# Stores of folded weight blocks held back, and the first pair's outputs moved to ScalarE

## The chip, the cores and the metric

One core of a Trainium2 chip runs the whole program. The metric is device microseconds of one execution, the median of three runs. The engines named here are PE (matmuls; PEld is its weight load), DVE (VectorE), ACT (ScalarE), POOL (GpSimd) and SP (SyncE, which here issues nearly every DMA). Each engine works through its instructions strictly in the order of the program.

## The reference

```python
# attention: q, k, v are (8, 8, 576, 64); the bias depends on head and positions alone
scores = q @ k.T / sqrt(64) + bias          # bias = relu(x @ w1 + b1) @ w2
attn = softmax(scores)
x = (attn @ v).transpose(0, 2, 1, 3).reshape(4608, 512)
# then a gated block, with no nonlinearity but the product
a = x @ moe_w1                               # (4608, 1024)
b = x @ moe_w2                               # (4608, 1024)
out = ((a * b) @ moe_w3) @ moe_w_out         # (4608, 512)
```

## The kernel before

The program first computes attention (about 440 us), then folds the two last weights into one, `moe_w3 @ moe_w_out` (1024 x 512, eight blocks of 128 rows, called `folded[ft]`), and then does the gated block. All fp32 factors are kept as a high and a low part, and a product is three matmuls (high by high, low by high, high by low).

The 4608 tokens are cut into six pairs of two tiles of 384 tokens (`CH`). For each pair the loop goes over the eight blocks `ft` of the hidden dimension; `n` counts the 48 steps, and `start(n)` is the planned time of a step.

**The first pair (`p == 0`, n = 0 to 7)** is computed plainly, since the weights of a cheaper scheme are still being made. In each step PE does, for tile `c` and then for tile `d`, two groups of twelve matmuls (`plain`, lines 802 to 814, into the PSUM banks X and Y) and nine matmuls of the down product of the step before (`down`, line 971, into the six banks `oc0` to `od2`). ACT copies X out (line 829), DVE multiplies Y by that copy (line 832, which frees Y for the next group), ACT and DVE split the product (lines 820 and 823). Beside this, ACT, DVE and POOL turn the int64 input weights `moe_w1` and `moe_w2` into fp32 parts (`fetch_w`, `base_w`, `sums_w`: the input lands in one of two tiles `wi` by a DMA of line 189, ACT reads it in line 197, DVE goes on in lines 207, 211 and 221, POOL in line 215), and load and combine the next pair's inputs (`split_x`: loads in lines 719 and 427, DVE lines 742 and 745, ACT line 751).

**The later pairs (n = 8 to 47)** use seven products in place of eight (`product`, line 785, in the order 2, 1, 6, 5, 7, 3, 4 of `AT_P`, all into X and Y) with copies and sums in `evict` (lines 836 to 854), and a seven-product form of the folded weight as well (`outward`, line 913, which reads tiles `fs` loaded from DRAM by line 911). The folded weight gets there through the DRAM arrays `f_d[k]`, k = 0 to 3, of eight slots each. `put_f(k)` (line 878) makes sums of two blocks and stores them (lines 899 and 900), and it also stores the plain blocks themselves: slot 0 and slots 3 and 6 for the high and the low part (lines 897 and 898), and slot 7 for one k (line 902).

**The last down products of the first pair** fall into step n = 8: nine matmuls for `d` at 2.1 us and nine for `c` at 8.4 us after its start (`AT_D`, line 770), among the seven products. `store` (line 987) copies each of the six banks to SBUF (tile `xB0`; two of the six copies on DVE, four on ACT) and SP stores them to `out0` (line 996). Only then are the banks and the SBUF under them free: the tiles `gh`, `gl` and `fs` of the later pairs and the banks of `outward` lie where they were (`first.close()`, `out_ps.close()` after the line 1135).

**What sets the order.** The steps of PE, ACT, DVE and POOL are put into a list with planned times (`at`, `put`), and `drive` emits them sorted by time; these four engines keep that order. SP is not among them: a list scheduler places a DMA on SP as soon as its model finds it ready, and of several ready ones the one emitted earlier. So the plain blocks' stores, which `put_f` emits last, are issued long before the rest of `put_f`, once the blocks exist. Eight semaphores serve all DMAs in turn.

Of the kernel before, what the change touches and what calls it, by code (L numbers as in the profile page):

```python
# [17 lines left out]
P = 128  # L18
# [112 lines left out]
def relpos_attention_moe(  # L131
# [18 lines left out]
    nc = tc.nc  # L150
# [3 lines left out]
    DO = out0.shape[1]  # L154
# [3 lines left out]
    NF = DF // P  # L158
# [4 lines left out]
    def f(ap):  # L163
        return ap.bitcast(F32)
# [80 lines left out]
    def put(plan, steps, *times):  # L245

        def one():
            next(steps, None)
        for at in times:
            plan.append((at, len(plan), one))  # L250
# [113 lines left out]
    for i in range(2):  # L364
        t = att.enter_context(tc.tile_pool(name=f"sums{i}", bufs=1)).tile([P, 64], F32, name=f"sums{i}")
# [112 lines left out]
    later = []  # L478
# [5 lines left out]
    later = [e[:3] for e in later]  # L484

    plan = [e for e in later if e[0] < 0.0]
    later = [e for e in later if e[0] >= 0.0]
# [6 lines left out]
    with ExitStack() as pro:  # L494
# [29 lines left out]
        def reach(G):  # L524

            return (G + 1) * GR - 1, S - 1 - G * GR
# [9 lines left out]
        for G in range(NGRP):  # L536
            n = max(reach(G)) + 1
# [60 lines left out]
    later = [e for e in later if e[0] >= t_s]  # L598
# [16 lines left out]
    f_d = [dram.tile([P, 8, 2, 2 * P], F32, name=f"f_d{k}") for k in range(NF // 2)]  # L615
    ups, base = {}, {}
    pairs = {p: dict(x=[None, None]) for p in range(NPR)}
# [53 lines left out]
    folded, wacc, w3 = {}, {}, {}  # L671
# [65 lines left out]
    def split_x(p, i):  # L737

        xr, rb, flat = load_x(p, i, xs, p == 1 and i == 0)
        yield  # L740
        for n in range(2):
            nc.vector.tensor_tensor(flat[:, n * W2:(n + 1) * W2], flat[:, n * W2:(n + 1) * W2], rb[:, n], op=ALU.mult)
            yield
        for o, x, y in ((4, 1, 0), (1, 3, 1), (5, 3, 4), (6, 2, 5)):
            nc.vector.tensor_tensor(xr[:, o], xr[:, x], xr[:, y], op=ALU.subtract)
            yield
        x = xb[(p + 1) % 2].tile([P, 2, 7, CH], F32R, name=f"xS{i}")
        pairs[p]["x"][i] = x
        places = (slice(1, 3), slice(2, 4)), (slice(0, 6, 5), slice(0, 2)), (slice(3, 5), slice(4, 6)), (6, 6)
        for o, y in places:  # L750
            nc.scalar.activation(x[:, 0, o], xr[:, y], AF.Copy)
            yield
        for o, y in places:
            nc.vector.tensor_tensor(x[:, 1, o], xr[:, y], f(x[:, 0, o]), op=ALU.subtract)
            yield
# [11 lines left out]
        dict(b=(9.80, "ACT"), B=(10.70, "DVE"), c=(11.20, "ACT"), C=(11.80, "DVE")),  # L767
        dict(a=(3.20, "ACT"), A=(4.40, "DVE")),
    )
    AT_D = {"d": 2.1, "c": 8.4}  # L770
    AT_U = {"c": 0.0, "d": 6.25}
    AT_G = {"p": 2.1, "g": 4.2, "h": 4.8, "l": 5.4}
    AT_D0 = {"c": 4.16, "d": 10.41}
# [104 lines left out]
    def put_f(k):  # L878

        (ha, la), (hb, lb) = folded[2 * k], folded[2 * k + 1]  # L880
        s = cva.tile([P, 4, 2 * P], F32, name="wi")
        fa, fb = [cva.tile([P, DO], F32, name="wmag") for i in range(2)]
        for o, x in ((fa, (ha, la)), (fb, (hb, lb))):
            nc.vector.tensor_tensor(o, f(x[0]), f(x[1]), op=ALU.add)
            yield
        a0, a1, b0, b1 = fa[:, 0:2 * P], fa[:, 2 * P:DO], fb[:, 0:2 * P], fb[:, 2 * P:DO]
        for o, x, y, op in (
            (2, a1, b1, ALU.add), (1, a0, a1, ALU.subtract), (0, s[:, 2], a0, ALU.subtract), (3, b0, s[:, 0], ALU.subtract),
        ):
            nc.vector.tensor_tensor(s[:, o], x, y, op=op)  # L890
            yield
        h = bg.tile([P, 4, 2 * P], F32R, name="big")
        nc.scalar.activation(h, s, AF.Copy)
        yield
        nc.vector.tensor_tensor(s.bitcast(F32R), s, f(h), op=ALU.subtract)
        for m, (x, a, b) in enumerate(((f(h), ha, hb), (s, la, lb))):
            nc.sync.dma_start(f_d[k][:, 0, m], f(a[:, 0:2 * P]))
            nc.sync.dma_start(f_d[k][:, 3:7:3, m], f(b).rearrange("p (s n) -> p s n", s=2))
            nc.sync.dma_start(f_d[k][:, 1:3, m], x[:, 0:2])
            nc.sync.dma_start(f_d[k][:, 4:6, m], x[:, 2:4])  # L900
            if k == order(NPR - 1)[-1] // 2:
                nc.sync.dma_start(f_d[k][:, 7, m], f(a[:, 2 * P:DO]))
        yield

    def load_f(k, j, n, plain=False):
        if plain:
# [80 lines left out]
    def store(j, t):  # L987
        if not spare:
            spare.append(x0p.tile([P, 2 * NT, DO], F32, name="xB0"))
        o = spare[0][:, NT * "dc".index(j) + t]  # L990
        if t == 1:
            nc.vector.tensor_copy(o, pairs[0]["o", j, t])
        else:
            nc.scalar.copy(o, pairs[0]["o", j, t])
        r0 = "cd".index(j) * CH + t * P
        nc.sync.dma_start(out0[r0:r0 + P, :], o)

    def at(time, step, *args):
        later.append((time, len(later), lambda: step(*args)))
# [6 lines left out]
    t_f = t_s + 11.12 + (2 * NF - 1) * PACE_F  # L1006
    for i in range(2 * NF):
        hf, t = divmod(i, NF)
# [28 lines left out]
    def start(n):  # L1037
        m = max(n - NF, 0)
        return t_f + STEP0 * min(n, NF) + STEP * m + EXTRA * (m % 2)

    def order(p):
        return [ft for m in range(NF // 2)[::1 if p % 2 == 0 else -1] for ft in (2 * m, 2 * m + 1)]

    for k in range(NF // 2):
        t0 = t_f + (101.0, 94.0, 80.5, 73.5)[k]
        put(later, put_f(k), *(t0 + d for d in (0.0, 0.9, 1.8, 2.4, 3.0, 3.6, 4.1, 5.6)))

    here, past = None, {}
    for n in range(NPR * NF):
        p, s = divmod(n, NF)  # L1050
        ft = order(p)[s]
        t0, t1 = start(n), start(n + 1)
        cs = dict(at=(p, ft), odd=n % 2)
        if p == 0:
            for j, u in AT_U.items():
                for m in range(2):
                    at(t0 + u + 2.08 * m, plain, cs, j, m)
                for k, d in AT_G.items():
                    if n == 0 and k + j == "gc":
                        d = AT_GC  # L1060
                    at(t0 + u + d, gate, cs, k + j)
            for j in "cd":
                t2 = t1 + (AT_D0 if n + 1 < NF else AT_D)[j]
                at(t2, down, cs, j)
                if ft == NF - 1:
                    for t in range(NT):
                        at(t2 + 2.1 + 0.6 * t, store, j, t)
            if ft in (4, 6):
                put(
                    later, split_x(1, int(ft > 4)), t0 - 6.0, t0 + 8.45, t0 + 9.45, *(t0 + 11.6 + 0.5 * d for d in range(4)),  # L1070
                    *(t1 + 2.0 + 0.55 * d for d in range(8)),
                )
            continue
        for k, d in AT_P.items():
            if n == NF and k == "4":
                d += 1.05
            at(t0 + d, product, cs, k)
        for k, d in AT_E.items():
            at(t0 + d, evict, cs, k)
        if s > 1:  # L1080
            put(later, load_w(p, ft), t0 - 2 * STEP + 0.3)
        if p < NPR - 1 and s in (0, 4):
            times = [start(n + d) + t for d, t in AT_X]
            put(later, split_x(p + 1, s // 4), start(n - 1) + 6.1, *times)
        if s % 2 == 0:
            continue
        m, k = s // 2, ft // 2
        last = n + 1 == NPR * NF
        for q in range(2):
            for key, (d, _) in (AT_SL if last else AT_S)[1 - q].items():  # L1090
                d = 5.4 + 0.1 * d if n == NF + 1 and key in "sS" else d
                at(start(n + (0 if last else q)) + d, sums_g, key)
        if last:
            at(past["2"] + 1.3, load_f, k, "1", 4, True)
            at(t0 + 4.5, join)
            for i, (o, w, g) in enumerate(((0, 0, 0), (2, 2, 0), (1, 0, 1), (3, 2, 1), (1, 3, 2), (3, 1, 2), (0, 3, 5), (2, 1, 5))):
                at(t0 + 10.55 + 1.05 * i, finish, o, w, g, i < 4)
                if i > 3:
                    at(t0 + 11.70 + 1.05 * i, last_of, p, o)
            continue  # L1100
        at(start(n + 1) + 0.50, sums_g, "R")
        for j, (q, d, e) in AT_O.items():
            tb = start(n + 1 + q)
            at(tb + d, outward, m, j)
            if e is not None:
                at(tb + e, gather, m, j, dict(zip("16753", (0, 1, 2, 3, 1)))[j])
            if here != k and j in F_BY:
                at(past[j] + 1.3 if j in past else start(NF + 1) + 5.5 + 0.05 * (q * STEP + d), load_f, k, *F_BY[j])
            past[j] = tb + d
        here = k  # L1110
        if m == NF // 2 - 1:
            for o, (q, d) in enumerate(((1, 0.2), (1, 7.6), (2, 1.1), (1, 4.5))):
                at(start(n + 1 + q) + d, complete, p, o)
# [91 lines left out]
```

## Time and profile before

| | |
|---|---|
| runs | 1051.98, 1052.49, 1053.36 us; median 1052.49 us |
| profiled execution | 1052.97 us, of which 1050.8 us lie from the first to the last instruction |
| busy, share of the span | PE 1020.6 us (97%), DVE 922.3 (88%), ACT 580.2 (55%), POOL 320.1 (30%) |
| granted clock of PE, mean | 0.995 |
| chain that ended last | PE 74%, DVE 10%, issue 7%, ACT 3%, DMA 3%, POOL 3% |
| DMA moved | 236.22 MB, 225 GB/s over the span |

A time in a row below is counted from the span's first instruction. In a timeline a row is one instruction, or several alike in a row (`x12`), with its start and its length; in square brackets stands how long the engine was idle before it and what ended that. A letter q behind an engine means its queue: a DMA issue, or a wait on semaphores. The first pair's steps run from about 493 to 595 us, step n = 8 from 595 us.

### The profile page before, as it was taken

Reading aid. Unit: us, or ns where it says so; the run is one execution under the profiler, and the core shown is the slowest. Engines: PE = TensorE matmul, PEld = TensorE weight load, DVE = VectorE, ACT = ScalarE, POOL = GpSimd, SP = SyncE. Lnnn points to the kernel's source line nnn. Section 1 sums busy time; section 2 is a strip of 40 time slices with the busy share of each in tenths; the row PEclk is TensorE's granted clock in tenths of the full one; section 3 lists DMA queues with packets and bytes.
Section 4 is the critical chain, followed back from the end, with each engine's and each line's share of the span. In section 5 each row is a group of like instructions: output and inputs, shape, how many; then the busy total and the mean of one; then the engine's idle time right before and its main releaser. Section 6 shows DMA issues by size and latency. Waiting matters only on the chain.

```text
span 1050.8 us, 34041 instructions
## 1 busy us (share of the span) xinstructions
PE 1020.6 (97%) x14094; PEld 837.6 (80%) x14094; DVE 922.3 (88%) x1616; ACT 580.2 (55%) x1250; POOL 320.1 (30%) x344
## 2 busy tenths in 40 slices
PE   7979999999999999999999989999999999999998
PEld 2346666666666666688899979999999999999998
DVE  8989999999999999998889958897887888787665
ACT  6957887877877788856454442334325333242421
POOL 0027885883778288674220000000000000000000
PEclk9989999999999999999999999999999999999999
DMA  7987777776776766367867788758648766764752
GB/s 215 298 236 230 209 213 222 217 211 200 211 220 186 202 189 192 115 167 239 321 220 279 242 327 291 267 181 317 230 159 300 261 219 216 277 227 146 250 196 90
DMA packets 109675, 236.22 MB, mean 225 GB/s; under 512 B 23376, under 2 KB 60624, under 8 KB 102736
## 3 DMA queue, kind: packets, MB, share of 16 engines
q1 hardware_dynamic: 109088, 234.02, 68.2%
q8 instruction: 111, 1.82, 0.7%
q14 instruction: 44, 0.36, 0.1%
q10 hardware_dynamic: 432, 0.02, 0.0%
HBM read 181.68 MB, written 52.31 MB: 223 GB/s over the span
## 4 chain that ended last, share of the span: by engine, by line
PE 74%; DVE 10%; issue 7%; ACT 3%; DMA 3%; POOL 3%; SPq 0%; DVEq 0%; ACTq 0%; POOLq 0%
PE X L797 16%; PE Y L797 12%; PE acc L442 11%; PE s L346 10%; PE ox L919 9%; DVE ts L357 4%; PE o L919 4%; PE bacc L566 3%; DVE pt L392 3%; PE X L811 3%; PE Y L811 2%; POOL w3s L688 2%; PE oc L980 1%; PE od L980 1%; DMA wi<-in_moe_w_dram 1%
## 5 line engine op out<-in xcount | busy, mean ns | idle before, releaser
L382 ACT ACTIVATE pp<-ts,mx 128x576 f32<-128x576 f32 x256 | 196.1, 767 | 39.9 <-DVE mx L357 38.9
L442 PE MATMUL acc<-pt,v 32*64 32x128 f32 (+1 forms) x9216 | 212.9, 294 | 2.4 <-issue 2.4
L442 PEld LDWEIGHTS acc<-pt,v 32*64 32x64 f32 x9216 | 160.0, 130 | 69.2 <-issue 44.8
L346 PE MATMUL s<-k,q 64*128 64x288 f32 (+1 forms) x1280 | 194.3, 441 | 6.7 <-DVE mx L357 4.7
L797 PE MATMUL X<-xS,wS 128*128 128x384 f32 x960 | 194.2, 336 | 2.7 <-DVE wos L840 1.3
L357 DVE CUSTOM_DVE_ANT_0 ts<-s,nb 128x576 f32<-128x576 f32 x256 | 182.4, 737 | 5.3 <-PE s L346 5.1
L392 DVE STREAM_TRANSPOSE pt<-pp 128x1152 f32<-128x1152 f32 x128 | 175.3, 1371 | 2.3 <-ACT pp L382 1.4
L797 PEld LDWEIGHTS X<-xS,wS 128*128 128x128 f32 x960 | 169.6, 188 | 4.2 <-ACT wos L844 1.9
L346 PEld LDWEIGHTS s<-k,q 64*128 64x128 f32 (+1 forms) x1280 | 91.1, 176 | 74.8 <-issue 35.8
L797 PE MATMUL Y<-xS,wS 128*128 128x384 f32 x720 | 145.4, 336 | 0.0
L844 ACT COPY wos<-X 128x384 f32<-128x384 f32 x80 | 38.4, 481 | 167.3 <-PE X L797 165.8
L797 PEld LDWEIGHTS Y<-xS,wS 128*128 128x128 f32 x720 | 127.0, 188 | 0.5 <-ACT wos L844 0.2
L334 POOL COPY v<-v 64x512 f32<-64x512 f32 (+1 forms) x160 | 87.5, 567 | 117.3 <-DMA v<-in_v_dram 98.3
L862 ACT ACTIVATE gh<-gr 128x768 fp32r<-128x768 f32 (+1 forms) x79 | 58.2, 760 | 81.4 <-DVE gr L867 69.2
L919 PE MATMUL ox<-gh,fs 128*128 128x384 f32 x380 | 97.0, 336 | 1.6 <-ACT gh L862 1.6
L930 DVE TENSOR_TENSOR sum<-ox,sum 128x768 f32<-128x768 f32 x75 | 71.7, 956 | 21.5 <-PE ox L919 21.5
L227 POOL TENSOR_TENSOR wmag<-wmag 128x512 int32<-128x512 int32 x72 | 74.8, 1039 | 5.8
L840 DVE TENSOR_TENSOR wos<-Y,wos 128x384 f32<-128x384 f32 x80 | 44.6, 557 | 35.6 <-ACT wos L844 20.5
L859 DVE TENSOR_TENSOR gl<-gr,gh 128x768 fp32r<-128x768 f32 (+1 forms) x79 | 65.5, 845 | 6.7 <-ACT gh L862 6.6
L919 PEld LDWEIGHTS ox<-gh,fs 128*128 128x128 f32 x380 | 68.6, 188 | 1.9 <-issue 1.9
L919 PE MATMUL ox<-gl,fs 128*128 128x384 f32 x190 | 63.7, 335 | 0.0
L207 POOL TENSOR_SCALAR wmag<-wmag 128x512 f32<-128x512 f32 x24 | 46.0, 1916 | 41.9 <-ACT wmag L197 41.9
(143 smaller groups left out, 1508.5 us busy)
## 6 DMA issues: line engine op xcount, KB each, us to landing
wS<-w_d SPq DMA_DIRECT2D x30, 1792.0 KB, 7.7
q<-in_q_dram SPq DMA_DIRECT2D x64, 288.0 KB, 4.1
fs<-f_d SPq DMA_DIRECT2D x15, 1024.0 KB, 5.8
w_d<-wS SPq DMA_DIRECT2D x8, 1792.0 KB, 6.8
v<-in_v_dram SPq DMA_DIRECT2D x96, 128.0 KB, 3.7
fs<-f_d SPq DMA_DIRECT2D x15, 768.0 KB, 4.5
nb_d<-bev SPq DMA_DIRECT2D x36, 295.5 KB, 4.0
k<-in_k_dram SPq DMA_DIRECT2D x64, 144.0 KB, 3.8
```

The source lines that it names most:

```text
L227: nc.gpsimd.tensor_tensor(d["bits"], d["bits"], d["bits"], op=ALU.add)
L334: nc.gpsimd.tensor_copy(t[64:128], t[0:64])
L346: nc.tensor.matmul(s[outs, hf, :HS], d[f"q{h}"][rows, q0:q0 + n], d[f"k{h}"][rows, :], start=True, stop=True,)
L357: nc.vector.tensor_tensor_reduce(out=halves(ts), in0=d.pop(("s", t))[:, :, :HS], in1=halves(NB[p, t]), op0=ALU.add, op1=ALU.min, scale=-1. ...
L382: nc.scalar.activation(d["p", ps][:, k * S:(k + 1) * S], ts, AF.Exp, bias=mx, scale=-1.0, accum_out=SUMS[u // 4 % 2][:, col:col + 1],)
L392: nc.vector.transpose(o, st[u].pop(("p", ts)))
L442: nc.tensor.matmul(acc[outs, a, c0:c0 + 32 * (t1 - t0)], d["v", b][rows, h], pt_[rows, t0:t1, 32 * b:32 * b + 32], start=(b == 0), stop=(b ...
L797: nc.tensor.matmul(acc, w[:, l, W_AT[n], i * P:(i + 1) * P], x[:, r, X_AT[n]], start=(k in "125" and i == 0 and m == 0), stop=(i == 1 and ...
L859: nc.vector.tensor_tensor(gl[:, o], gr[:, x], f(gh[:, o]), op=ALU.subtract)
L862: nc.scalar.activation(gh[:, o], gr[:, x], AF.Copy)
L919: nc.tensor.matmul(bank[:, e, :CH], fs[n // 4][:, n % 4, l, e * P:(e + 1) * P], r[:, G_AT[j]], start=i == 0 and (j in "15" or (j in "24" a ...
L930: nc.vector.tensor_tensor(sums[o], x, sums[o], op=ALU.add)
```

## The change

The stores of the plain blocks leave `put_f` and form a step list of their own, `put_h(k)`, planned at `t_f + 31 + 7k` and 2.6 us later (`t_f` is the planned start of step 0). Before each store, POOL copies two columns of each block onto themselves (128 x 2 elements), so the store must wait for POOL's place in the plan. The last down product of `c` moves from 8.4 to 5.25 us in step 8, and the products 7, 3 and 4 of that step 1.05 us back. The six output copies are all done by ACT, and ACT issues their stores.

```diff
-    AT_D = {"d": 2.1, "c": 8.4}
+    AT_D = {"d": 2.1, "c": 5.25}
...
         nc.vector.tensor_tensor(s.bitcast(F32R), s, f(h), op=ALU.subtract)
-        for m, (x, a, b) in enumerate(((f(h), ha, hb), (s, la, lb))):
+        for m, x in enumerate((f(h), s)):
+            nc.sync.dma_start(f_d[k][:, 1:3, m], x[:, 0:2])
+            nc.sync.dma_start(f_d[k][:, 4:6, m], x[:, 2:4])
+        yield
+
+    def put_h(k):
+
+        for m, (a, b) in enumerate(zip(folded[2 * k], folded[2 * k + 1])):
+            for o in (a, b):
+                nc.gpsimd.tensor_copy(o[:, 0:DO:2 * P], o[:, 0:DO:2 * P])
             nc.sync.dma_start(f_d[k][:, 0, m], f(a[:, 0:2 * P]))
             nc.sync.dma_start(f_d[k][:, 3:7:3, m], f(b).rearrange("p (s n) -> p s n", s=2))
-            nc.sync.dma_start(f_d[k][:, 1:3, m], x[:, 0:2])
-            nc.sync.dma_start(f_d[k][:, 4:6, m], x[:, 2:4])
             if k == order(NPR - 1)[-1] // 2:
                 nc.sync.dma_start(f_d[k][:, 7, m], f(a[:, 2 * P:DO]))
-        yield
+            yield
...
         o = spare[0][:, NT * "dc".index(j) + t]
-        if t == 1:
-            nc.vector.tensor_copy(o, pairs[0]["o", j, t])
-        else:
-            nc.scalar.copy(o, pairs[0]["o", j, t])
+        nc.scalar.copy(o, pairs[0]["o", j, t])
         r0 = "cd".index(j) * CH + t * P
-        nc.sync.dma_start(out0[r0:r0 + P, :], o)
+        nc.scalar.dma_start(out0[r0:r0 + P, :], o)
...
         t0 = t_f + (101.0, 94.0, 80.5, 73.5)[k]
+        put(later, put_h(k), *(t_f + 31.0 + 7.0 * k + 2.6 * d for d in range(2)))
         put(later, put_f(k), *(t0 + d for d in (0.0, 0.9, 1.8, 2.4, 3.0, 3.6, 4.1, 5.6)))
...
-            if n == NF and k == "4":
+            if n == NF and k in "734":
                 d += 1.05
```

## Rows read from the trace of the kernel before

**Rows 1.** Timeline of PE, first pair and steps 9 and 10.

```profile
504.46 3.77 PE L811 MATMUL X<-xB,wS 128*128 128x384 f32 x12 [1.99 <-ACT wos L829]
508.06 1.47 PE L811 MATMUL Y<-xB,w2k 128*128 128x384 f32 x6
...
558.99 1.32 PE L811 MATMUL Y<-xB,w2k 128*128 128x384 f32 x6
...
609.39 1.32 PE L797 MATMUL X<-xS,wS 128*128 128x384 f32 x6 [0.62 <-ACT wos L844]
...
616.13 1.33 PE L797 MATMUL X<-xS,wS 128*128 128x384 f32 x6 [1.34 <-DVE wos L840]
...
621.60 0.59 PE L919 MATMUL ox<-gh,fs 128*128 128x384 f32 x2 [1.61 <-ACT gh L862]
```

**Rows 2.** Timeline of ACT, first pair and step 8.

```profile
502.82 0.67 ACT L197 ACTIVATE wmag<-wi 128x512 f32<-128x512 f32 x1 [1.18 <-DMA wi<-in_moe_w_dram]
...
553.46 0.66 ACT L197 ACTIVATE wmag<-wi 128x512 f32<-128x512 f32 x1 [1.46 <-DMA wi<-in_moe_w_dram]
...
605.65 0.59 ACT L994 COPY xB<-oc 128x512 f32<-128x512 f32 x1 [0.80 <-PE oc L980]
608.86 0.48 ACT L844 COPY wos<-X 128x384 f32<-128x384 f32 x1 [2.62 <-PE X L797]
```

**Rows 3.** Timeline of SP's queue: DMA issues.

```profile
495.44 0.37 SPq L189 DMA_DIRECT2D wi<-in_moe_w_dram  x1
495.91 1.33 SPq L897 DMA_DIRECT2D f_d<-w3s  x1
...
502.70 0.97 SPq L898 DMA_DIRECT2D f_d<-w3s  x2
...
547.77 0.60 SPq L427 DMA_DIRECT2D rb<-r_m  x1
548.47 0.53 SPq L189 DMA_DIRECT2D wi<-in_moe_w_dram  x1
...
602.94 2.34 SPq L996 DMA_DIRECT2D out_dram<-xB  x3
...
608.36 2.07 SPq L996 DMA_DIRECT2D out_dram<-xB  x3
...
612.98 0.87 SPq L911 DMA_DIRECT2D fs<-f_d  x2
```

**Rows 4.** Stretches: length; busy PE, PEld, DVE, ACT, POOL; clock; DMA share; GB/s.

```profile
504.00:508.00 4.00, 3.54 (x12) 3.26 (x12) 4.00 (x7) 0.41 (x2) 1.02 (x2) 0.63 1.05 356
...
600.00:603.00 3.00, 3.00 (x18) 2.81 (x17) 2.95 (x5) 2.30 (x4) 0.00 (x0) 1.00 0.59 187
...
618.00:621.00 3.00, 1.84 (x9) 1.19 (x8) 2.91 (x6) 2.19 (x4) 0.00 (x0) 1.00 1.03 421
```

**Rows 5.** Timeline of DVE, first pair.

```profile
507.46 0.55 DVE L832 TENSOR_TENSOR wos<-Y,wos 128x384 f32<-128x384 f32 x1
...
558.39 0.55 DVE L832 TENSOR_TENSOR wos<-Y,wos 128x384 f32<-128x384 f32 x1
```

**Rows 6.** Line 742, 555 to 558.6 us: count, ns min/median/max, first and last start.

```profile
L742 DVE TENSOR_TENSOR xr<-xr,rb x2: 952/1498/2044, 555.6 to 556.4; 128x768 f32<-128x768 f32 x2
```

**Rows 7.** Timeline of POOL, first pair.

```profile
539.06 0.11 POOL L717 MEMSET xr<- 128x2 f32 x1
542.31 1.29 POOL L215 TENSOR_TENSOR big<-big,wmag 128x512 int32<-128x512 int32 x1 [3.14 <-DVE big L221]
```

**Rows 8.** Line 919, 619 to 622 us, in the form of rows 6.

```profile
L919 PEldq EVENT_SEMAPHORE  x5: 51/51/2420, 618.7 to 621.5; - x5
```

**Rows 9.** Line 911 at 613.4 us, the second of the first two loads of `fs`.

```profile
L911 SPq DMA_DIRECT2D fs<-f_d x1: 493/493/493, 613.4 to 613.4; - x1
...
DMA to landing us min/median/max: 9.7/9.7/9.7
```

**Rows 10.** DMA issues by line: KB each, median us to landing.

```profile
out_dram<-xB SPq DMA_DIRECT2D x6, 256.0 KB, 3.1
```

## The prediction, made before the changed kernel ran

> **What bounds the kernel now.** I read the busy shares first: PE is busy for 97% of the span, so a change can only win where PE stands still, or lose by making it stand still elsewhere. The timeline of PE over the two stretches that the change touches shows its stops [rows 1]: 1.99 us at 504.46, in step 1, and after the change to seven products 0.62, 1.34 and 1.61 us at 609.39, 616.13 and 621.60 (a fourth, of 0.6, lies between them). From 508.06 to 607 it shows none: PE goes through steps 1 to 8 without a stop. Then I asked of each stop what ended it, in the timelines of the engine named and of SP's queue, and of the stretch without stops how near it is to one.
>
> *The stop at 504.46.* ACT's copy of X stands behind a read of `wi`, which waited 1.18 us for its DMA [rows 2]. That DMA was issued at 495.44, and twelve stores of plain blocks follow it by 506 [rows 3]. PE then ran at a mean granted clock of 0.63 for 4 us [rows 4], the lower of its two levels (1.2 GHz) in most of them, so that twelve matmuls took 3.77 us. But the next group, at 508.06, needs bank Y, which DVE frees with the multiplication of 507.46 to 508.01 [rows 1, 5], and DVE is busy for 4.00 of the 4.00 us before 508 [rows 4]. DVE, not the DMA, set the time of 508.06.
>
> *The stretch without stops.* The group at 558.99 also needs Y, and DVE freed it at 558.39 + 0.55 = 558.94 [rows 1, 5]: slack 0.05 us. Back from there DVE runs through two multiplications of `split_x` [rows 6] to work that began when ACT read `wi` at 553.46, and ACT had waited 1.46 us for that DMA [rows 2]. It was issued at 548.47, right behind the fourteen loads of `split_x`, of which the last took 0.60 us of SP [rows 3]; these wait for a POOL instruction that ended at 539.17 [rows 7]. By the timelines POOL's instruction hangs, through DVE and ACT, on a copy of X, so this chain moves with PE's own pace and has no slack against it.
>
> *The stop at 621.60.* The profile names ACT, but PE's queue stood for 2.42 us in one wait, from 618.7 to 621.1, and four short waits behind it fill the rest [rows 8]. What ended it is the first load of `fs`: both loads were issued from 612.98 on [rows 3], and the second, smaller by a quarter, landed at 613.4 + 9.7 = 623.1 [rows 9], with the DMA engines full at 421 GB/s [rows 4]; its 0.79 MB at that rate are 1.9 us, so the first was there at about 621.2. The loads waited for the last output stores, issued up to 610.43 and landing 3.1 us after issue [rows 3, 10].
>
> **The change part by part.**
>
> *A. The stores leave 482 to 513 us: 0.* Eighteen stores, 3.4 MB, go from beside the weights' DMAs. The `wi` of 495.44 stands ahead of most of them in the same queue; what its landing gains frees ACT, but not DVE, and PE is at 508.06 by DVE. Ends: 0, and a gain of 3.4 if all of the stop (1.99) and the slow clock came off (six matmuls take 1.32 at 558.99, twelve about 2.4, against 3.77: 1.4). I take 0, since the DVE row is the nearest to PE's next instruction.
>
> *B. The stores come back later: +2.0.* In POOL's order the copies of k = 2 stand behind the memset of 539.06 (two) and behind the instruction of 542.31 (two) [rows 7]; those of k = 3 there as well, but their stores are emitted after the `wi` of 548.47 and are placed after it. The four stores of k = 2 (planned at 45 and 47.6 us after `t_f`) are emitted before that `wi` (49.2) while SP still has loads to issue, so all four go between the loads and `wi`. A store costs SP 0.97 / 2 = 0.49 us where the queue flows, 1.33 us where it is backed up [rows 3]; 4 x 0.49 = 1.96. Ends: 0 (the scheduler places `wi` first) and 5.3 (4 x 1.33). The loads ahead are small, so I take the low price. The wait then stands on ACT at its read of `wi`; behind it queue the copy of X and, on DVE, the multiplication that frees Y; PE loses what exceeds 0.05 us. A store that waits for its copy holds SP, and `wi` loads queue behind it; for k = 0 and 1 (ten stores, at 525 to 533) those `wi` land several us before ACT reads them, so they are hidden; ends 0 and 1.
>
> *The sixteen POOL copies: 0.* Nearest row: the memset of 128 x 2 at 0.11 us [rows 7], 1.8 us in all on an engine that is 30% busy. Of the two multiplications of line 742 one took 0.95 us and one, beside POOL's work, 2.04 [rows 6]: DVE and POOL hold each other up. The Trainium skill ("SBUF — State Buffer", "SBUF: two separate sides") says that a DVE operation with two SBUF inputs and a GpSimd operation that reads SBUF exclude each other for a whole instruction; by it each copy could cost DVE its own length, 1.8 us if all fell on the chain. By the rows none of the sixteen falls on it, so 0; ends 0 and 1.8.
>
> *C. The outputs on ACT, the last `c` product sooner: -1.6.* SP loses six issues, 2.34 + 2.07 us [rows 3]. The `c` banks are done 3.15 - 1.05 = 2.1 us sooner, and the `d` copies no longer wait for SP until 602.94. With ACT's copies and issues in a row (below) the last store is issued at about 608.4, lands at 611.5, and `fs` is issued then, 1.5 us sooner than 612.98. The DMA engines were only 0.59 busy from 600 to 603 [rows 4], and that room is filled too, so the first `fs` is there by 619 to 620, when PE's product before it ends (621.60 - 1.61 = 619.99). All 1.61 go; late next is the seven-product chain itself. The stops of 0.62, 0.6 and 1.34 stay: PE waits there for copies of what it has just made. That two copies leave DVE saves nothing, since DVE waits for PE there. Ends: 0 and -1.6.
>
> *D. ACT's load in step 8: +0.2.* Added: two copies of 0.59 [rows 2] and six issues of 0.69 to 0.78 (2.07 and 2.34 for three) [rows 3], 5.5 us, of which one issue falls before 600. Against these 4.8 us stand ACT's idle times: 2.62 before 608.86 and 0.80 before 605.65 [rows 2], 0.70 from 600 to 603 [rows 4], and I count 0.5 between; late by 0.2. A store that waits for its copy holds ACT; behind it queue the copies that PE waits for, the one at 608.86 with nothing else for PE to do. Ends: 0, and 1.25 if each issue takes 0.9. The product 3 comes a whole down product later, so its copy of Y keeps 1 us of slack.
>
> Sum: 0 + 2.0 - 1.6 + 0.2 = +0.6 us; the profiled execution's 1052.97 (span 1050.8 and 2.2 around it) becomes 1053.6. That execution is 0.48 above the median of 1052.49, so I predict 1053.1 for the median.
>
> **The rivals.**
>
> 1. *The stores of k = 2 are hidden* (B = 0): SP places `wi` before them, or its landing gains what they cost. For it: ACT's 1.46 us of waiting are all DMA. Against: the emission order, and 0.05 us of slack. 1052.49 - 1.4 = 1051.1.
> 2. *The first stop is worth something* (A): DVE, its input earlier, frees Y sooner, and the clock stays up. For it: the stop and the slow matmuls are there. Against: DVE's 4.00 of 4.00. With 1.5 of the 3.4 and B = 0: 1049.6.
> 3. *The held stores jam SP* (slower): behind a larger store still in the queue, each of the four takes 1.33 us. B = 5.3, less 1.4: 1056.4. It decides slower, by the bound below, from 0.9 us a store on (4 x 0.9 - 1.4 = 2.2). Against: the issues just ahead took 0.60, not 1.33.
> 4. *`fs` lands no sooner* (C = 0): the DMA engines are full, the bytes ahead of `fs` are the same, and the stop is paid by bytes, not by the last store. For it: 421 GB/s at 618 to 621 [rows 4]. 1052.49 + 2.0 + 0.2 = 1054.7. The Trainium skill says the same ("DMA: Bandwidth & Descriptors", "Issuing engines are not separate DMA queues"): DMAs of all issuers run on the same sixteen engines, and another issuer saves only the time of issuing. The share of 0.59 before 603 speaks against it.
>
> **How the numbers follow.** The forecast 48% (its own range 1052.1 to 1053.9: B from 1.0 to 2.6, and 0.2 for D's spread), rival 1 20%, rival 2 12%, rival 3 12%, rival 4 8%. About 0.2%, 2.1 us, is what a measurement can tell here. Faster by more than that (under 1050.4): nearly all of rival 2 and a little of 1, 0.16. Slower (over 1054.6): rival 3, most of 4, the forecast's tail, 0.21. Else 0.63. The range of 1050.3 to 1055.6 leaves out two thirds of each of rivals 2 and 3 and some tail.
>
> **What would show it.** A: PE's first Y group of step 1 still starts at about 508, whatever stands before it. B: four f_d stores between the last load and `wi`, and stops of PE of about 2 us in all in step 5, at 557 to 561. C: PE's wait in line 919 gone, `fs` issued 1 to 2 us sooner in step 9. D: ACT's copy at the start of step 9 less than 0.5 us after its product. Wrong would be: no stop in step 5, or Y free before 507.

## The result: half a per cent slower, and the profile after

The changed kernel took 1058.05 us (median of 5 runs, 1057.28 to 1060.29) against 1052.49 for the kernel before beside it: a ratio of 1.0051, 95% interval 1.0026 to 1.0075. Forecast were 1053.1, with 1055.6 as the upper end.

**How the two traces are laid side by side.** No kernel here changes anything ahead of 480 us, yet the same group of matmuls in step 1 starts up to 5.6 us apart in the profiled executions (the table below). So spans are not compared, but shifts: the start of a group of PE after, less its start before, and where that shift grows. A time less the shift at its place is called a time by the clock of the kernel before. The changed kernel's PE, in steps 1, 5 and 9:

```profile
498.62 2.38 PE L811 MATMUL X<-xB,wS 128*128 128x384 f32 x12 [0.60 <-ACT wos L829]
...
505.03 2.38 PE L811 MATMUL X<-xB,wS 128*128 128x384 f32 x12 [1.60 <-ACT wos L829]
509.03 1.31 PE L811 MATMUL Y<-xB,w2k 128*128 128x384 f32 x6 [1.62 <-DVE wos L832]
...
559.05 2.38 PE L811 MATMUL X<-xB,wS 128*128 128x384 f32 x12 [1.41 <-ACT wos L829]
562.95 1.32 PE L811 MATMUL Y<-xB,w2k 128*128 128x384 f32 x6 [1.51 <-DVE wos L832]
...
613.17 1.32 PE L797 MATMUL X<-xS,wS 128*128 128x384 f32 x6 [0.57 <-ACT wos L844]
...
623.11 2.29 PE L797 MATMUL X<-xS,wS 128*128 128x384 f32 x6 [5.49 <-DVE wos L840]
...
628.49 0.58 PE L926 MATMUL ox<-gh,fs 128*128 128x384 f32 x2
```

Against [rows 1]: the Y group of step 1 is 0.97 us later (509.03 for 508.06), that of step 5 3.96 (562.95 for 558.99), the first use of `fs` 6.89 (628.49 for 621.60), and the shift is still 6.9 at the last matmul. The 0.97 were there before step 1: in both kernels the Y group of step 1 comes 7.97 us after the Y group ahead of it (500.09 before, 501.06 after, timeline of PE). So step 1 gave nothing, the way to step 5 cost 3.0 us, and the way through steps 8 and 9 another 2.9: 5.9 in all. In step 9 two old stops are gone (1.61 at `fs`, and one of 0.6) and a new one of 5.49 stands where 1.34 stood; the six matmuls behind it took 2.29 us instead of 1.33.

**Step 5.** SP's queue:

```profile
548.78 0.60 SPq L427 DMA_DIRECT2D rb<-r_m  x1
549.48 0.53 SPq L906 DMA_DIRECT2D f_d<-w3s  x1
...
551.17 0.41 SPq L907 DMA_DIRECT2D f_d<-w3s  x1
551.68 0.50 SPq L189 DMA_DIRECT2D wi<-in_moe_w_dram  x1
...
605.41 0.67 SPq L661 DMA_DIRECT2D wS<-w_d  x1
613.79 0.36 SPq L897 DMA_DIRECT2D f_d<-big  x1
...
620.25 0.81 SPq L918 DMA_DIRECT2D fs<-f_d  x2
```

Four held stores stand between the last load and `wi`, as forecast; they take 549.48 to 551.68, 2.2 us. ACT and DVE, on the same timeline view, in steps 5 and 9:

```profile
557.42 0.66 ACT L197 ACTIVATE wmag<-wi 128x512 f32<-128x512 f32 x1 [4.62 <-DMA wi<-in_moe_w_dram]
...
620.29 0.84 ACT L862 ACTIVATE gh<-gr 128x768 fp32r<-128x768 f32 x1 [4.23 <-DMA f_d<-wi]
...
621.16 0.96 DVE L859 TENSOR_TENSOR gl<-gr,gh 128x768 fp32r<-128x768 f32 x1 [6.59 <-ACT gh L862]
```

ACT's read of `wi` comes 5.7 us after the issue (557.42 less 551.68), where it was 5.0 [rows 2, 3]. That the four stores moving beside it are the reason is argued. 2.2 and 0.7 are 2.9 of the 3.0.

**Step 9.** The stop of 5.49 hangs on DVE, that on ACT's copy into `gh`, and that on the DMA that stores `f_d` from `wi`: `gh` lies where those tiles were. These stores went out at 613.79; before, SP issued them between two groups of output stores, from 605.34. Ahead of them stands a row that no row of before answers to in this place: a load of `wS` (1.8 MB) at 605.41. Before, SP issued it in step 6. The kernel before, in the timeline of SP's queue:

```profile
579.11 0.67 SPq L661 DMA_DIRECT2D wS<-w_d  x1
...
605.34 0.63 SPq L899 DMA_DIRECT2D f_d<-big  x1
```

The windows show the same 1.8 MB leaving a slack stretch and entering a full one. The columns are those of [rows 4]; first the kernel before, then the changed one:

```profile
570.00:580.00 10.00, 10.00 (x56) 9.61 (x55) 8.10 (x16) 2.87 (x5) 0.00 (x0) 1.00 0.93 342
...
605.00:610.00 5.00, 4.38 (x24) 3.97 (x23) 3.24 (x6) 1.07 (x2) 0.00 (x0) 1.00 1.03 355
620.00:625.00 5.00, 3.40 (x20) 3.44 (x21) 2.91 (x4) 2.52 (x4) 0.00 (x0) 1.00 1.04 421
```

```profile
570.00:580.00 10.00, 10.00 (x53) 9.21 (x52) 8.80 (x18) 3.32 (x6) 0.00 (x0) 1.00 0.61 163
...
605.00:610.00 5.00, 5.00 (x27) 4.60 (x26) 2.45 (x4) 3.30 (x6) 0.00 (x0) 1.00 1.08 356
620.00:625.00 5.00, 1.89 (x6) 1.89 (x7) 3.77 (x6) 3.57 (x5) 0.00 (x0) 0.58 0.98 410
```

From 570 to 580, 342 less 163 GB/s over 10 us are 1.8 MB. From about 605 to 625 the DMA engines were already at a share of 1 before; bytes that are added there should make what follows late: 1.8 MB at the 410 to 421 GB/s of the last rows are 4.3 to 4.4 us, an estimate. SP's waits name the other half of the picture (engine, line, what was waited for, us):

```profile
SPq L897 <- DMA out_dram<-xB: 7.7, 1, 7.7
```

SP stood 7.7 us in front of the `f_d` stores until one of ACT's output stores, issued at 605.24, had landed. They read other tiles; both use the same one of the eight DMA semaphores. Two theories follow. Theory 1: the hold (the stores made to wait for POOL's copies) makes both stalls, since it moved the load of `wS`. Theory 2: ACT's stores make the second.

### The profile page after: what moved, and what is told of

Same layout as the page of the kernel before. It is cut to its first block, busy times and chain, and to the rows that moved or that the text cites. A ratio compares the mean times of both kernels' runs of the same rounds, so it can differ in the third digit from the quotient of the medians.

```text
span 1058.4 us, 34048 instructions
## 1 busy us (share of the span) xinstructions
PE 1021.2 (96%) x14094; PEld 839.2 (79%) x14094; DVE 921.8 (87%) x1614; ACT 581.0 (55%) x1252; POOL 325.9 (31%) x360
## 4 chain that ended last, share of the span: by engine, by line
PE 76%; DVE 9%; issue 6%; DMA 3%; POOL 2%; ACT 2%; DVEq 0%; ACTq 0%; SPq 0%; POOLq 0%
PE X L797 15%; PE acc L442 13%; PE s L346 12%; PE Y L797 12%; PE ox L926 9%; PE o L926 4%; DVE ts L357 4%; PE bacc L566 3%; DVE pt L392 2%; PE Y L811 2%; PE X L811 2%; POOL w3s L688 2%; PE od L987 1%; PE oc L987 1%; DMA wS<-w_d 1%
## 5 line engine op out<-in xcount | busy, mean ns | idle before, releaser
L859 DVE TENSOR_TENSOR gl<-gr,gh 128x768 fp32r<-128x768 f32 (+1 forms) x79 | 65.4, 844 | 10.3 <-ACT gh L862 10.2
```

The costliest lines, as they stand in the source:

```text
L859: nc.vector.tensor_tensor(gl[:, o], gr[:, x], f(gh[:, o]), op=ALU.subtract)
```

## The experiments

Each was timed in five rounds beside the kernel before (6 to 12 runs); ratios are to that, with 95% intervals. Of the one profiled execution of each the table gives the shift against the kernel before at the Y group of step 1 (508.06), and what PE lost or won from there to the Y group of step 5 (558.99), and from there to a group near the end (1043.89). What the last two columns add up to lies within 1.4 us of what the ratio says; a smaller difference between two kernels rests on one trace of each.

| kernel | ratio | shift at step 1 | to step 5 | from step 5 on |
|---|---|---|---|---|
| changed | 1.0051 (1.0026 to 1.0075) | +0.97 | +2.99 | +2.95 |
| e1 hold alone | 1.0069 (1.0046 to 1.0091) | +0.10 | +3.20 | +3.98 |
| e2 no hold | 0.9989 (0.9971 to 1.0008) | -0.70 | -0.03 | -1.08 |
| e3 hold sooner | 1.0054 (1.0034 to 1.0075) | +1.02 | +4.85 | +1.03 |
| e4 SP stores | 1.0066 (1.0042 to 1.0089) | +2.89 | +3.04 | +4.26 |
| e5 late `wS` alone | 1.0034 (1.0015 to 1.0053) | +1.51 | +0.13 | +3.28 |
| e6 later k = 2, 3 | 1.0040 (1.0026 to 1.0054) | -0.71 | -0.25 | +4.73 |
| e7 two pairs held | 1.0028 (1.0013 to 1.0042) | +4.19 | +0.67 | +2.73 |
| e8 `wS` by ACT | 1.0092 (1.0064 to 1.0120) | +2.13 | +3.15 | +5.71 |
| e9 hold spread | 1.0081 (1.0059 to 1.0103) | +0.50 | +7.78 | +2.10 |
| e10 sooner `c` alone | 1.0014 (1.0000 to 1.0028) | -1.43 | +0.13 | +0.07 |
| e11 half of `wS` late | 1.0028 (1.0007 to 1.0049) | +0.16 | +0.52 | +1.39 |
| e12 `fs` ahead of `wS` | 0.9976 (0.9958 to 0.9994) | +0.78 | +0.31 | -2.21 |

**e1: the hold alone.**

```diff
 # the changed kernel, with
-    AT_D = {"d": 2.1, "c": 5.25}
+    AT_D = {"d": 2.1, "c": 8.4}
 # and store(), "734" as in the kernel before
```

> The kernel before with the held stores alone (put_h and the shortened put_f; the outputs of the first pair copied, placed and stored as before, the down product c as before). Two stalls were found in the changed kernel: 3.0 us in step 5, and 3 us net in step 9. Theory 1 (the hold makes both: four stores ahead of wi in step 5, and SP's order changed so that the load of wS for the third step of the next pair goes out at 605.4 instead of 579.1, just ahead of the outputs and of f_d): stops of 2.9 us in step 5, and a stop of 4 to 6 us at the copies of gh in step 9, with ScalarE storing nothing; 1057 to 1059 us. Theory 2 (the stall of step 9 comes from ScalarE's stores, which share DMA engines and semaphores with SP's): the stop of step 5 alone, step 9 as in the kernel before with 1.34 and 1.61; 1055.5 us.

Both stalls came, with ACT storing nothing. PE of e1:

```profile
558.40 2.38 PE L811 MATMUL X<-xB,wS 128*128 128x384 f32 x12 [1.63 <-ACT wos L829]
562.29 1.31 PE L811 MATMUL Y<-xB,w2k 128*128 128x384 f32 x6 [1.50 <-DVE wos L832]
...
623.46 2.29 PE L797 MATMUL X<-xS,wS 128*128 128x384 f32 x6 [5.38 <-DVE wos L840]
```

The load of `wS` was issued at 604.48, three outputs behind it, and ACT's `gh` waited 3.94 us for an output store; an output behind the load took up to 9.3 us to land, where 3.4 was the longest before. The hold costs 3.2 and 4.0 us; ACT's stores are not needed for either.

**e2: everything but the hold.**

```diff
 # the kernel before, with
+    AT_D = {"d": 2.1, "c": 5.25}
...
+        nc.scalar.copy(o, pairs[0]["o", j, t])
...
+        nc.scalar.dma_start(out0[r0:r0 + P, :], o)
...
+            if n == NF and k in "734":
```

> The changed kernel without the hold: stores of plain blocks as in the kernel before, but the outputs copied and stored by ScalarE and the down product c sooner. The load of wS stands at 579 again. Theory 1 (the hold makes both stalls): no stop in step 5, no long stop in step 9, the 1.61 us stop at the first load of fs gone; 1051 us (1050.5 to 1052.5). Theory 2 (ScalarE's stores make the stall of step 9): a stop of 4 to 5 us at gh's copies and slow clock behind it; 1055 us (+2.5 to +3.5).

Neither stall, and `wS` at 578.29. The stop at `fs` shrank from 1.61 to 1.21, at 619.79; that of 1.34 went, and one of 1.10 came at 613.17; 1.1 us won in the trace, and a ratio whose interval still holds 1. By the clock of the kernel before, `fs` was issued only 0.4 us sooner (611.87 with a shift of -0.73, for 612.98).

```profile
613.17 1.33 PE L797 MATMUL Y<-xS,wS 128*128 128x384 f32 x6 [1.10 <-ACT wos L844]
...
619.79 0.58 PE L919 MATMUL ox<-gh,fs 128*128 128x384 f32 x2 [1.21 <-issue]
```

e1 and e2 add up: 3.2 + 4.0 - 1.1 is 6.1, and the change as a whole lost 5.95.

**e3: the hold sooner.**

```diff
-        put(later, put_h(k), *(t_f + 31.0 + 7.0 * k + 2.6 * d for d in range(2)))
+        put(later, put_h(k), *(t_f + 31.0 + 3.0 * k + 2.6 * d for d in range(2)))
```

> The changed kernel with one number changed: the held stores of block pair k planned at 31 + 3k instead of 31 + 7k, so that all of them stand in SP's queue ahead of the loads of split_x, and the load of wS stands right behind the first f_d stores again (579). Theory 1: both stalls gone; 1051 us, unless the sixteen stores, now together at 525 to 545, make a wi load late there (then up to 1054). Theory 2: the stall of step 5 gone and that of step 9 still there; 1055 us.

Half a miss. The load of `wS` is early again and the stop of 5 us in step 9 is gone, as theory 1 has it. But the jam (stores one behind another, each over 1 us of SP), which had been set down at up to 3 us, cost 4.85. SP of e3:

```profile
540.12 1.20 SPq L906 DMA_DIRECT2D f_d<-w3s  x1
...
542.67 1.13 SPq L189 DMA_DIRECT2D wi<-in_moe_w_dram  x1
...
554.50 0.53 SPq L189 DMA_DIRECT2D wi<-in_moe_w_dram  x1
```

Five stores in a row take 1.0 to 1.2 us each (536.58 to 541.42), both `wi` behind them come late, and PE stands 3.28 us at 560.97.

**e4: SP stores the outputs again.**

```diff
-        nc.scalar.dma_start(out0[r0:r0 + P, :], o)
+        nc.sync.dma_start(out0[r0:r0 + P, :], o)
```

> The changed kernel with the six outputs of the first pair stored by SP again (hold, copies on ScalarE and the sooner c product kept). SP's order is then: the late load of wS, three outputs, the last f_d stores, three outputs. Theory 1 (hold): both stalls stay; 1057 to 1059 us. Theory 2 (ScalarE's stores): step 9 as in the kernel before, step 5's stop alone; 1055 us.

Both stalls stay: the 5.49 us are 6.23 here. PE of e4:

```profile
625.86 2.29 PE L797 MATMUL X<-xS,wS 128*128 128x384 f32 x6 [6.23 <-DVE wos L840]
```

Theory 2 is out: taking ACT's stores away from the changed kernel does not help it. In the trace it is 1.3 us worse; the intervals of the two ratios overlap.

**e5: a late load of `wS`, by its edit nothing else.**

```diff
 # the kernel before, with
+        if (p, t) == (1, 4):
+            nc.vector.memset(f(w[:, 0, 0, 0:2]), 0.0)
...
-            put(later, load_w(p, ft), t0 - 2 * STEP + 0.3)
+            put(later, load_w(p, ft), t0 - 2 * STEP + (3.0 if n == NF + 2 else 0.3))
```

> The kernel before with nothing but a late load of wS: VectorE writes two columns of the tile for the third step of the second pair at step 8's time, and SP loads it behind that, at about 602, between the f_d stores of block pair 1 and the first outputs, where the hold had put it (the hold itself and ScalarE's stores are not in this kernel). Theory 1 (this load's place makes the stall of step 9): no stop in step 5, a stop of 5 to 6 us at gh's copies in step 9 with the slow clock behind it; 3.5 to 5 us slower than the kernel before. Rival (the stall of step 9 follows from the 3 us that step 5 lost, which shift the engines against the transfers): no change, within 0.5 us of the kernel before.

Without a held store the stall of step 9 is there, 3.3 us net. The outputs behind the load took up to 10.2 us to land (3.4 at most before), and SP stood 3.2 us in front of the next outputs for the landing of `wS`, whose semaphore the first of them shares. The queue changed in one more place: SP took some loads of `rb` and `xr` ahead of 595 us in another order, where PE shows no stop. SP and PE of e5:

```profile
601.38 0.82 SPq L663 DMA_DIRECT2D wS<-w_d  x1
602.29 2.97 SPq L998 DMA_DIRECT2D out_dram<-xB  x3
...
611.89 1.69 SPq L998 DMA_DIRECT2D out_dram<-xB  x3
```

```profile
621.46 2.29 PE L799 MATMUL X<-xS,wS 128*128 128x384 f32 x6 [5.04 <-DVE wos L842]
```

**e6: the stores of k = 2 and 3 behind the `wi` of step 5.**

```diff
-        put(later, put_h(k), *(t_f + 31.0 + 7.0 * k + 2.6 * d for d in range(2)))
+        put(later, put_h(k), *(t_f + (31.0, 38.0, 53.0, 54.0)[k] + 2.6 * d for d in range(2)))
```

> The changed kernel with the held stores of block pairs 2 and 3 planned at 53 and 54 us after t_f (before: 45 and 52), so that they follow the wi of step 5 in SP's queue; the load of wS still comes late, at about 603. Theory 1: the two stops of step 5 gone, the stop of 5 to 6 us in step 9 stays; 2.5 to 4 us slower than the kernel before. Rival (step 9 follows from step 5): both stalls gone; 1 us faster than the kernel before.

The mirror image of e3. SP issues `wi` at 547.72, before the stores, and PE goes through step 5 without a stop; the load of `wS` stays late and so does the stop of step 9:

```profile
603.09 0.67 SPq L661 DMA_DIRECT2D wS<-w_d  x1
```

```profile
619.29 2.29 PE L797 MATMUL X<-xS,wS 128*128 128x384 f32 x6 [6.54 <-DVE wos L840]
```

The two stalls are separate: e6 has the second alone, e3 the first without the long stop of the second. In e6 eight stores stand behind `wi`, and all but the first take about 1.1 us of SP each (those issued from 549.37 to 556.83); PE pays nothing for that, since no `wi` is behind them.

**e11: half of the load late.**

```diff
 # e5, with the load in two halves, the second behind the memset
+            nc.sync.dma_start(f(w[:, 0].rearrange("p s n -> p (s n)")), w_d[t][:, 0:14 * P])
+            nc.vector.memset(f(w[:, 1, 0, 0:2]), 0.0)
+            nc.sync.dma_start(f(w[:, 1].rearrange("p s n -> p (s n)")), w_d[t][:, 14 * P:])
```

> The kernel before with half of that one load of wS (its low parts, 0.9 MB) held to 602 as the whole was in the run with nothing but a late wS (3.5 us slower, a long stop at gh's copies in step 9); the other half goes out early. Theory 1 (paid by bytes: 1.8 MB at 0.415 GB/ms are 4.4 us): half the bytes, so the stop shrinks by 2.2 us, to about 3 us, and the kernel is 1 to 1.7 us slower than before. Rival (paid by the order alone: anything that stands there holds the outputs back until it has landed, or the semaphore that it shares stops SP): the stop stays within 1 us of that of the whole load; 3 us slower.

The stop grew over the 1.34 of before by 2.13, with the whole load by 3.70; net 1.4 against 3.3. In the traces it goes by bytes; the timed ratios (1.0028 and 1.0034) do not tell half from whole. By which of two ways the bytes do it stays open: an output behind the load took up to 7.3 us to land (10.2 with the whole load), and SP stood 1.3 us for the load's semaphore (3.2). PE of e11:

```profile
618.91 1.50 PE L802 MATMUL X<-xS,wS 128*128 128x384 f32 x6 [3.47 <-DVE wos L845]
```

**e7: two pairs held.**

```diff
+                if k < 2:
                     nc.gpsimd.tensor_copy(o[:, 0:DO:2 * P], o[:, 0:DO:2 * P])
```

> The changed kernel with only block pairs 0 and 1 held; the eight stores of pairs 2 and 3 wait for no copy and go out at 500 to 515. SP's order has the wi of step 5 right behind the loads and the load of wS at 579 again. Both theories on the stall of step 9 expect it gone, and that of step 5 too; what it tells is whether a hold can be had for nothing: 1 us faster than the kernel before (the stop of 1.61 gone, as with ScalarE's stores alone), or, if the ten held stores jam SP as the eighteen did in the run with all of them sooner (1.0 to 1.2 us each there), up to 3 us slower.

A miss on step 9: no stop at `gh`, but one at `fs`. PE and SP of e7:

```profile
627.60 0.58 PE L927 MATMUL ox<-gh,fs 128*128 128x384 f32 x2 [3.93 <-issue]
```

```profile
590.62 0.88 SPq L427 DMA_DIRECT2D rb<-r_m  x1
595.73 0.33 SPq L719 DMA_DIRECT2D xr<-x_d  x1
...
607.33 0.58 SPq L897 DMA_DIRECT2D f_d<-big  x1
...
616.98 0.96 SPq L919 DMA_DIRECT2D fs<-f_d  x2
```

SP's order differs once more: one `rb` load stands ahead of the `xr` load that waits for its memory until 595.73, where before there were three. Two loads at 0.6 us or more slip behind it, and the `f_d` stores go out at 607.33, 6.6 us later than before (600.71), of which the shift at step 5 explains 4.9. Small loads that slip into the full stretch thus count as well; that they are all of the 2.7 us is argued, not shown.

**e8: ACT issues that load of `wS`, early.**

```diff
-        nc.sync.dma_start(f(w.rearrange("p h s n -> p (h s n)")), w_d[t])
+        (nc.scalar if (p, t) == (1, 4) else nc.sync).dma_start(f(w.rearrange("p h s n -> p (h s n)")), w_d[t])
 # planned at start(NF - 1) - 2.0
```

> The changed kernel with that one load of wS issued by ScalarE at about 580 instead of by SP at 605; everything else as changed. Theory 1: the stall of step 9 gone with the stop of 1.61 too, that of step 5 stays; 1.5 to 2.5 us slower than the kernel before, so 3 us faster than the changed kernel. Rival (step 9 follows from step 5, or from ScalarE's stores): both stay; 5 us slower.

A clear miss, the slowest of all, although `wS` went out at 587.24. ACT of e8:

```profile
609.64 0.48 ACT L844 COPY wos<-X 128x384 f32<-128x384 f32 x1 [5.94 <-DMA xr<-x_d]
...
625.23 0.84 ACT L862 ACTIVATE gh<-gr 128x768 fp32r<-128x768 f32 x1 [5.50 <-DMA out_dram<-xB]
```

The first wait is that of ACT's own store in front of this copy: its semaphore had last been given to a load of SP's, and ACT stood until that landed, with the copies that PE needs behind it. The second: `gh` lies over `xB`, and the last output store, issued at 616.19 just behind the next 1.8 MB of `wS`, took 8.9 us to land, where their median was 3.0. So theory 2's mechanism exists, though the changed kernel is no faster without ACT's stores (e4).

**e9: the hold spread out.**

```diff
-        put(later, put_h(k), *(t_f + 31.0 + 7.0 * k + 2.6 * d for d in range(2)))
+        put(later, put_h(k), *(t_f + 20.0 + 6.0 * k + 2.6 * d for d in range(2)))
```

> The changed kernel with the held stores of block pair k planned at 20 + 6k instead of 31 + 7k: in SP's queue they stand in groups of three or four between the wi loads of steps 2 to 4, none between the loads of split_x and wi, and the load of wS is early again; but, as in the run with two pairs held, two of the rb loads of step 7 stand behind an xr load that waits for its memory. Theory 1 (the stall of step 9 is paid by the bytes that move into a stretch, 603 to 624 us, in which the DMA engines are full): no stop of 5 us; within 0.5 us of the run with ScalarE's stores alone, 1 us faster than before, if only wS's 1.8 MB count; and 1.5 to 3 us slower than before if, as with two pairs held, loads that slip by 2 us into that stretch count as well. If the groups of four jam SP as eight in a row did (1.0 to 1.2 us each), a wi is late in step 5 as well: 3 to 5 us slower.

The price in step 9 came as with two pairs held (2.1 us, no stop of 5 at `gh`). Up to step 5 it was worse than expected, 7.8 us, and half of it (3.8 us by the group that starts at 520.94 in the kernel before) for a reason that neither theory had. PE and POOL of e9:

```profile
519.63 0.50 PE L987 MATMUL od<-w3s,ghd 128*128 128x512 f32 x1 [2.15 <-POOL w3s L905]
```

```profile
518.92 1.75 POOL L905 CAST w3s<-w3s 128x2 fp32r<-128x2 f32 x6
```

POOL's copy writes two columns of a block that PE's down product reads: PE waits for a copy whose only use is to delay a store, and runs at a mean granted clock of 0.83 from 515 to 525.

One thing stays open. In e3, e7 and e9 the load of `wS` is early and the stop of 5 us is gone, and still they lose 1.0 to 2.7 us from step 5 on, where e2, without a hold, wins 1.1. A late `wS` makes most of the second stall (3.3 us in e5, of the 4.0 in e1); but a hold that leaves it early still costs 2 to 4 us there, and what takes them was not isolated.

**e10: the sooner `c` product alone.**

```diff
 # the kernel before, with
+    AT_D = {"d": 2.1, "c": 5.25}
...
+            if n == NF and k in "734":
```

> The kernel before with the last c product one slot sooner (and products 7 and 3 placed behind it), nothing else: no hold, outputs copied by ScalarE and VectorE and stored by SP as before. SP's order of DMAs is that of the kernel before. With ScalarE storing, the gain was 1.1 us. If it came from the banks being done sooner: the first output stores and so fs 1 us sooner, the 1.61 us stop halved or gone, 0.5 to 1.1 us faster than before. If it came from ScalarE issuing beside SP: no gain, within 0.3 us of before.

No gain. PE and SP of e10:

```profile
557.69 1.34 PE L811 MATMUL Y<-xB,w2k 128*128 128x384 f32 x6
...
614.78 2.04 PE L797 MATMUL X<-xS,wS 128*128 128x384 f32 x6 [2.31 <-DVE wos L840]
```

```profile
611.86 0.91 SPq L911 DMA_DIRECT2D fs<-f_d  x2
```

In the span `fs` was issued 1.1 us sooner (612.98 before), but PE's step 5 was 1.3 us sooner too (558.99 before): against PE, `fs` did not come sooner. The stop there fell to 0.64 (620.38), behind a stop of 2.31 that stands in place of 1.34. So the gain of e2 needs the copies and stores on ACT. Which of the two, no run shows without the hold; with it, ACT's copies do worse with SP's stores (e4) than with ACT's own (the changed kernel), by 1.3 us in the trace.

**e12: e2, and `fs` ahead of the next `wS`.**

```diff
 # e2, with
+        if (p, t) == (1, 5):
+            nc.vector.memset(f(w[:, 0, 0, 0:2]), 0.0)
...
-            put(later, load_w(p, ft), t0 - 2 * STEP + 0.3)
+            put(later, load_w(p, ft), t0 - 2 * STEP + (7.0 if n == NF + 3 else 0.3))
```

> ScalarE's stores and the sooner c product without the hold (the run that came out 1.1 us faster in its trace), and the next load of wS (1.8 MB, issued at 607.7 there, ahead of both fs loads) held by a write of VectorE until it stands behind the fs loads in SP's queue. Theory 1 (step 9 is paid by the bytes ahead in a stretch where the DMA engines are full): fs lands 3 to 4 us sooner, at about 616, the 1.21 us stop at the first use of fs goes; 1 us faster than without this, 2 us faster than the kernel before (1051.5 against 1053.6). Rival (the order in which memory comes free sets fs, or the load of wS, now 5 us later, is late for its own step): no gain, or 1 to 3 us slower than without this, with a stop of the product that reads that wS at about 636.

The size came out as theory 1 said, 2.2 us in all, and this version beats both kernels: 1052.16 us against 1053.94 for the kernel before beside it, with an interval below 1. The path differs: four `rb` loads went ahead of `fs` too, which was issued only at 613.83, by the clock of the kernel before no sooner than in e2, so a stop of 0.74 remains. Its first use still came 1.1 us sooner than in e2 by that clock (620.48 less 1.09, against 619.79 plus 0.73), not the 3 to 4 expected: with `wS` behind it, `fs` landed sooner after its issue. PE and SP of e12:

```profile
620.48 0.59 PE L921 MATMUL ox<-gh,fs 128*128 128x384 f32 x2 [0.74 <-DMA fs<-f_d]
```

```profile
613.83 0.94 SPq L913 DMA_DIRECT2D fs<-f_d  x2
615.47 2.11 SPq L663 DMA_DIRECT2D wS<-w_d  x2
```

## Why the prediction was wrong

**A, the stores leave 482 to 513: 0. Right.** With the stores gone, PE's stop behind ACT's copy shrank (1.99 to 1.60) and the clock stayed up (2.38 us for twelve matmuls instead of 3.77), and the Y group came at the same place: from the X group that starts at 498.62 after and at 497.64 before, 10.41 us after and 10.42 before. The row of before:

```profile
497.64 2.38 PE L811 MATMUL X<-xB,wS 128*128 128x384 f32 x12 [0.59 <-ACT wos L829]
```

DVE is named in the row of 509.03. In e1 and e6, which hold as well, the Y group also comes 7.97 us behind the Y group ahead of it.

**B, the stores come back: +2.0. Mechanism right, size 3.0.** The four stores, `wi` behind them, X and Y late, all as forecast; 2.2 us of SP instead of 1.96, and 0.7 us of slower landing that the term did not have. e6 takes this away (-0.25).

**POOL's copies: 0 on this path, but each was priced too low.** By their line they took 0.18 to 0.66 us, median 0.40, against the 0.11 of the memset [rows 7]:

```profile
L905 POOL CAST w3s<-w3s x16: 179/396/662, 525.9 to 546.3; 128x2 fp32r<-128x2 f32 x16
```

The bound considered DVE; e9 shows that PE can be the one that waits.

**C, -1.6: this is the step that failed.** It said: "the last store is issued at about 608.4, lands at 611.5, and `fs` is issued then, 1.5 us sooner than 612.98". The last store was issued at 610.63, by the clock of the kernel before (3.96 less) at 606.7, so ACT's copies and issues were not what failed. The landing was: the output stores took 7.8 us in the median (3.1 before, [rows 10]). SP stood for one of them, the `f_d` stores went out 4.5 us later than before by the same clock, and `fs` waited for these to land as well (2.2 us among SP's waits). It was issued at 620.25, by that clock at 616.3: 3.3 us later than 612.98, not 1.5 sooner. That PE's wait at `fs` is gone (628.49) is no success of C; PE itself comes there 2.9 us later. What went before `fs` was not the DMAs of the kernel before, but 1.8 MB more. The sum had no term for that, because B followed the held stores only to their neighbours: SP is placed by a list scheduler, and eighteen stores that come some 40 us later (POOL's first copy is at 525.9, the first store stood at 482) gave the whole queue behind them another order. e5 makes the loss with that one load alone, e11 half of it with half the bytes, e6 with the load but without B. Why the scheduler moved the load was not settled: it did whenever held stores stood behind the loads of `split_x` (the changed kernel, e6) and did not when all stood ahead (e3, e7, e9).

Freed from the hold, C and D together are worth -1.1 (e2) where -1.4 was forecast, but that the two are near is luck. The last store of e2 was issued when C had said (607.74, by the clock of the kernel before 608.5), but took 4.0 us to land; `fs` came 0.4 us sooner, not 1.5, and 0.4 of the 1.61 went, not all. e10 says that the banks done sooner bring nothing by themselves.

**D, ACT's load: +0.2. Not seen, and small.** An issue cost ACT 0.34 us (0.41 at most), half of what SP's rows had suggested, and the stop behind it was 0.57 (0.62 before). What D did not have is that an issue can stand for another engine's DMA, as ACT's did in e8.

**The rivals.** Rival 4 (`fs` no sooner, paid by bytes) had the mechanism and 8%; it kept "the bytes ahead of `fs`" the same, and they were not. The Trainium skill ("DMA: Bandwidth & Descriptors", "Issuing engines are not separate DMA queues") says that DMAs of all issuers run on the same sixteen engines and interleave. This trace agrees: ACT's small stores took 7.8 us to land beside SP's `wS`, 3.1 before. Rival 3's price of 1.33 us a store did not come in step 5 (0.55 each), but nearly did where stores follow each other (1.0 to 1.2 in e3).

## What to carry to other kernels

When a DMA is moved in a queue that a scheduler places, compare the whole order of that queue before and after, not the neighbourhood: here a large load went out 26 us later (22 by the clock of the kernel before), in a stretch whose DMA engines were full. In such a stretch price every transfer that enters by bytes over the measured rate (a first estimate: 4.4 us for `wS`, where e5 lost 3.3), and look for those that can leave it: letting `fs` pass the next `wS` was worth as much in the trace (1.1 us) as e2's other changes together. And a dummy write that delays a store also orders every reader of the tile behind it.

## What the hardware showed that was not expected

- A DMA issue can stand for a transfer that it has nothing to do with, since eight semaphores go round over SP's and ACT's DMAs: SP stood 7.7 us in the changed kernel, ACT 5.94 in e8.
- The longer stops of step 9 were paid again behind them: six matmuls took 1.33 us behind a stop of 1.34, but 2.04 behind one of 2.31 (e10) and 2.29 behind all those of 5.04 to 6.54; behind 3.47 (e11) the first six took 1.50 and the next six 2.12. In the changed kernel the granted clock from 620 to 625 was 0.58, between full speed and the lower of the two levels (1.2 GHz, 0.5).
- A copy of 128 x 2 elements on POOL took 0.40 us in the median (0.18 to 0.66); the one memset of that shape took 0.11.
